# Retention and a bilinear feed-forward on one core: loading k and q of two pairs first, scaling the second pair on GpSimd, transposing q by parity

## The chip, the cores and the metric

The kernel runs on one core of one Trainium2 chip. Its time is device microseconds (us) of one execution; a time of a kernel is the median of its runs.

## The reference

A recurrent retention (linear attention with a decay for each head) is followed by a bilinear feed-forward. B = 4, H = 8, S = 768, D = 64; the feed-forward goes from 512 to 1536 and back.

```
gamma = 1 - 2 ** (-5 - arange(H));  scale = 1 / sqrt(D)
for t in range(S):
    state = gamma * state + outer(k[:, :, t], v[:, :, t])      # per batch and head, D x D
    y[:, :, t] = scale * q[:, :, t] @ state
x = y.transpose(0, 2, 1, 3).reshape(B * S, H * D)              # 3072 x 512
out = ((x @ w_a) * (x @ w_b)) @ w_out                          # float32
```

Inputs and outputs are float32.

## The kernel before

The 3072 rows are 24 slots of 128. The decay is put into k and q beforehand (`scaled`, line 210: k times one table of exponentials, q times another), so that the recurrence becomes plain linear attention: masked scores inside a chunk of rows (intra) plus q times a running state (inter).

The first six slots, all of batch 0, are worked as three *pairs* of 256 rows. A pair is loaded with even and odd rows side by side in one partition, so its two halves are a parity (`par`) each; c is the upper or lower half of the partitions, that is the first or second 128 rows of the pair. For a pair u the steps are:

- `casts2` scales k and q to bf16 (`kqb`) and casts v (`vb`)
- `flip2` transposes k or q on TensorE (line 384) through a PSUM tile `tp` and copies it to `kT2` or `qT2`
- `scores2` multiplies them (line 400, `at`), and VectorE multiplies the result by a mask (line 406, `aT`)
- `update2` adds k times v to the running state (line 419, `st`), and `keep_state` copies it for use as weights (line 428, `gbd`, on ScalarE)
- `intra2` and `inter2` sum masked scores times v and q times the state into two PSUM tiles `y` (lines 448 and 436), one for each c
- `leave2` copies these to `xt`, the feed-forward's input

The feed-forward `ffn_a`, `ffn_g` (lines 482 and 492) multiplies 128 columns of `w_a` or `w_b` by up to 512 rows of `xt`; ScalarE copies the one result (`asb`), VectorE multiplies the other by it (`ht`). `ffn_out` (line 519) is the second matrix product. The rows are cut into eight blocks (`TILES`); the first has the first two pairs, so the feed-forward cannot start until pair 0 and 1 have left. The 18 other slots are worked between feed-forward tiles.

Weights are loaded as float32 and cast by GpSimd (`cast_w`, `cast_o`). All loads are issued on one queue (SP) in the order of the list `LOADS`. `warm` issues matmuls of a zero tile whose result nobody uses (line 468), as filler on TensorE.

The order on every engine is the order in which the program text issues the work: `seq` chains each instruction to the one before it on its engine. PSUM tiles come from pools: `psff` has three buffers used in turn (tag `ff`: transposes, one of the two score sets, fillers, feed-forward), `psat` has one each for `at`, `y0` and `y1`, `psst` one for the state. A new tile waits until the old one in its buffer has been read.

Of the kernel before, what the change touches and what calls it, by code (L numbers as in the profile page):

```python
# [17 lines left out]
ON_PE = 8  # L18


LOADS = "p0 p1 w0 w1 w2 w3 w4 p2 w5 o0 o1 o2 o3 o4 o5 s6 s7 s8 s9 s10".split()


@with_exitstack
def kernel(
# [10 lines left out]
    nc = tc.nc  # L36
# [55 lines left out]
    def load_pair(u):  # L92
        for nm, src in (("k", k), ("q", q), ("v", v)):
            f = raw.tile([P, H, 2, D], F32, tag=nm + "f", name=nm + "f")
            s = src[0, :, 2 * u * P : 2 * (u + 1) * P, :].rearrange("h (p two) d -> p h two d", two=2)
            seq(nc.sync.dma_start(out=f, in_=s))
            for par in range(2):
                raws[nm, 2 * u + par] = f[:, :, par, :]

    def load_w(j):  # L100
        for nm, src in (("a", moe_w_a), ("b", moe_w_b)):
# [13 lines left out]
    def issue_loads(n):  # L115
        for _ in range(min(n, len(pending))):
            what = pending.pop(0)
            {"p": load_pair, "s": load_slot, "w": load_w, "o": load_o}[what[0]](int(what[1:]))


    kqb = {}
    issue_loads(6)
    zero = const.tile([P, 2 * P], F32, name="zero")
    seq(nc.vector.memset(zero, 0.0))  # L124
    lgr = const.tile([P, 1, H], F32, name="lgr")
    bq = const.tile([P, 1], F32, name="bq")
# [51 lines left out]
    def cast(engine, dst, src):  # L178
        if engine is nc.scalar:
            seq(nc.scalar.copy(dst, src))  # L180
        else:
            seq(engine.tensor_copy(dst, src))  # L182
# [182 lines left out]
    kT2, qT2 = {}, {}  # L365

    def casts2(u, on):
        for t in (2 * u, 2 * u + 1):
            new_nat(t)
        for (i, par), eng in on.items():  # L370
            scaled(eng, 2 * u + par, i)
        for t in (2 * u, 2 * u + 1):
            cast(nc.gpsimd, vb[t], raws["v", t])

    def flip2(u, i, on):
        if i == 0 and u not in kT2:
            kT2[u] = tra.tile([P, 2, HP, P], BF16, tag="kT2", name="kT2", bufs=2)
        if i == 1 and u not in qT2:
            qT2[u] = tra.tile([P, HP, P, 2], BF16, tag="qT2", name="qT2", bufs=2)
        for pars, eng in on:  # L380
            tp = psff.tile([P, 2, HP, P], BF16, tag="ff", name="tp")[:, : len(pars)]
            for m, par in enumerate(pars):
                for hp in range(HP):
                    seq(nc.tensor.transpose(tp[:, m, hp, :], kqb[2 * u + par][:, i, hp, :, :], ident))  # L384
            if i == 0:
                cast(eng, kT2[u][:, pars[0] : pars[0] + len(pars)], tp)
            else:
                cast(eng, qT2[u][:, :, :, pars[0]], tp[:, 0])

    def scores2(u, par, ff=False):  # L390
        t = 2 * u + par
        if not ff:
            both = psat.tile([P, 2, HP, P], F32, tag="at", name="at")
            at = [both[:, r] for r in range(2)]
        else:
            at = [psff.tile([P, HP, P], F32, tag="ff", name=f"at{r}") for r in range(2)]
        for hp in range(HP):
            for c in range(2):
                for r in range(2):
                    seq(nc.tensor.matmul(at[r][half(c), hp, :],  # L400
                                         kT2[u][half(r), par, hp, half(c)],
                                         qT2[u][half(r), hp, half(c), :],
                                         start=True, stop=True, skip_group_check=True))
        aT[t] = tra.tile([P, 2, HP, P], BF16, tag="aT", name="aT")
        for r in range(2):
            seq(nc.vector.tensor_tensor(aT[t][:, r], at[r], masks[par].to_broadcast([P, HP, P]),  # L406
                                        op=ALU.mult))
# [19 lines left out]
        for r in range(2):  # L427
            seq(nc.scalar.copy(gbd[1 - c][half(r), :, half(r)], state[0][half(r), :, :]))

    def inter2(u):  # L430
        for c in range(2):
            if (u, c) == (0, 0):
                continue
            for r in range(2):
                for hp in range(HP):
                    seq(nc.tensor.matmul(ys[u][c][half(hp % 2), 2 * r + hp // 2, :],
                                         gbd[c][:, hp, half(r)],
                                         qT2[u][:, hp, half(c), :], start=False, stop=False,
                                         skip_group_check=True))

    def intra2(u, par, begin):
# [10 lines left out]

    def leave2(u, on):
        J, i = where[2 * u]
        if i == 0:
# [9 lines left out]
    def warm(n, pool, tag):  # L465
        idle = pool.tile([P, 4 * P], F32, tag=tag, name="idle")
        for _ in range(n):
            seq(nc.tensor.matmul(idle[:, : 2 * P], zero[:, :P], zero, start=True, stop=True,  # L468
                                 skip_group_check=True))

    ht = {}
# [60 lines left out]
    K, Q = 0, 1  # L532
# [36 lines left out]
    ffn_a(0, 0, W2, 2 * W2)  # L569
    ffn_g(0, 0, 0, W2)  # L570
    ffn_g(0, 1, 0, W2)
    ffn_a(0, 1, W2, 2 * W2)
# [99 lines left out]
```

## Time and profile before

| | |
|---|---|
| median of 3 runs | 231.59 us (230.83 to 231.66) |
| the profiled execution's own time | 231.07 us |
| its span in the profile | 229.2 us |
| busy: TensorE, VectorE, ScalarE, GpSimd | 222.2, 97.9, 95.0, 78.0 us |
| moved by DMA | 39.19 MB, mean 171 GB/s |

In the rows PE is TensorE's matmuls, PEld its weight loads, DVE VectorE, ACT ScalarE, POOL GpSimd, SP the queue that issues the loads. L with a number is a line of the kernel; a helper (line 182 for copies on VectorE and GpSimd, 180 for those on ScalarE) stands for all its callers, so the tile names tell which copy it is. "xN" is a count; what stands in brackets is the engine's idle time before the instruction and what ended it. All times start with the span.

### The profile page before, as it was taken

How to read it: one execution, taken by the hardware profiler on the slowest of the kernel's cores; microseconds unless marked ns; L12 is line 12 of the kernel's file. 1: busy time of each engine (PE TensorE's matmuls, PEld its weight loads, DVE VectorE, ACT ScalarE, POOL GpSimd, SP SyncE). 2: the span in 40 equal slices, each digit the busy share in tenths (PEclk: the TensorE clock that was granted, in tenths of full speed). 3: DMA queues.
4: the chain of work that ended last, by engine and by line, in shares of the span. 5: the costliest groups of instructions: out<-in, count | busy, mean ns of one | idle time of the engine just before them, and what ended most of it. 6: DMA issues, size and time to landing. Idle time of an engine off the chain costs nothing.

```text
span 229.2 us, 6225 instructions
## 1 busy us (share of the span) xinstructions
PE 222.2 (97%) x2606; PEld 132.4 (58%) x2606; DVE 97.9 (43%) x193; ACT 95.0 (41%) x207; POOL 78.0 (34%) x101
## 2 busy tenths in 40 slices
PE   7989999999999999999989999999999999999994
PEld 6767445687446885885865454454445444444444
DVE  3695357645505552553565247460237310243300
ACT  3464426342427445445365336362335432433222
POOL 5568778787444444317086205000000000000000
PEclk9999999999999999999999999999999999999999
DMA  6999999999599998999999938002200002100022
GB/s 183 347 381 382 358 308 391 286 255 241 148 224 250 304 236 172 247 259 219 233 241 211 255 46 94 0 3 99 84 3 3 0 25 115 46 0 1 3 92 92
DMA packets 94011, 39.19 MB, mean 171 GB/s; under 512 B 73888, under 2 KB 89504, under 8 KB 93984
## 3 DMA queue, kind: packets, MB, share of 16 engines
q1 hardware_dynamic: 93840, 38.68, 67.0%
q8 instruction: 20, 0.33, 0.6%
q10 hardware_dynamic: 144, 0.13, 0.2%
q14 instruction: 7, 0.06, 0.1%
HBM read 28.31 MB, written 6.29 MB: 151 GB/s over the span
## 4 chain that ended last, share of the span: by engine, by line
PE 93%; DVE 4%; issue 1%; ACT 0%
PE o L519 27%; PE g L492 27%; PE a L482 27%; PE idle L468 3%; PE y L325 2%; PE y L336 1%; PE at L284 1%; DVE aT L406 1%; PE st L261 1%; DVE qT L182 1%; PE at L400 1%; DVE kqb L210 1%; PE y L448 1%; PE tp L384 1%; DVE aT L290 1%
## 5 line engine op out<-in xcount | busy, mean ns | idle before, releaser
L494 DVE TENSOR_TENSOR ht<-g,asb 128x256 bf16<-128x256 f32 (+1 forms) x98 | 53.7, 549 | 98.6 <-PE g L492 83.1
L482 PE MATMUL a<-xt,wa_bf 128*128 128x256 bf16 (+1 forms) x392 | 78.0, 323 | 1.3 <-DVE sums L275 0.5
L492 PE MATMUL g<-xt,wb_bf 128*128 128x256 bf16 (+1 forms) x392 | 77.5, 323 | 0.1
L485 ACT CAST asb<-a 128x256 bf16<-128x256 f32 (+1 forms) x98 | 46.4, 473 | 72.6 <-PE a L482 71.9
L519 PE MATMUL o<-wo_bf,ht 128*128 128x512 bf16 (+2 forms) x312 | 63.8, 363 | 0.0
L482 PEld LDWEIGHTS <-wa_bf 128*128 128x128 bf16 x392 | 37.6, 98 | 26.2 <-issue 1.0
L492 PEld LDWEIGHTS <-wb_bf 128*128 128x128 bf16 x392 | 38.3, 98 | 24.1 <-issue 0.4
L519 PEld LDWEIGHTS <-ht 128*128 128x128 bf16 x312 | 29.0, 98 | 31.4
L180 ACT COPY osb<-o 128x512 f32<-128x512 f32 (+2 forms) x25 | 14.1, 565 | 39.8 <-PE o L519 35.6
L210 POOL TENSOR_TENSOR kqb<-kf,ktab 128x512 bf16<-128x512 f32 x22 | 22.9, 1044 | 18.7 <-DMA kf<-in_k_dram 16.6
L182 POOL CAST vb<-vf 128x512 bf16<-128x512 f32 x24 | 15.4, 649 | 35.2 <-PE y L336 11.2
L210 POOL TENSOR_TENSOR kqb<-qf,qtab 128x512 bf16<-128x512 f32 x18 | 18.8, 1043 | 1.9 <-DMA qf<-in_q_dram 1.9
L180 ACT CAST gst<-sums 128x256 bf16<-128x256 f32 x33 | 12.9, 406 | 4.0 <-DVE sums L275 2.0
L275 DVE TENSOR_TENSOR sums<-st,sums 128x256 f32<-128x256 f32 x30 | 12.7, 423 | 1.4
L468 PE MATMUL idle<-zero 128*128 128x256 f32 x30 | 10.6, 493 | 1.3 <-DVE zero L124 1.3
L290 DVE TENSOR_TENSOR aT<-at,mask 128x512 bf16<-128x512 f32 x18 | 11.5, 679 | 0.0
L345 ACT CAST xt<-y 128x512 bf16<-128x512 f32 x18 | 9.7, 588 | 0.7 <-PE y L336 0.7
L468 PEld LDWEIGHTS idle<-zero 128*128 128x128 f32 x30 | 6.8, 245 | 2.5 <-DVE zero L124 1.2
L406 DVE TENSOR_TENSOR aT<-at,mask 128x512 bf16<-128x512 f32 x12 | 7.4, 681 | 1.0 <-PE at L400 1.0
L182 POOL CAST wb_bf<-wstb 128x1024 bf16<-128x1024 f32 (+1 forms) x7 | 6.9, 993 | 2.6 <-DMA wstb<-in_moe_w_b_dram 2.6
L182 POOL CAST wo_bf<-wsto 128x1024 bf16<-128x1024 f32 x6 | 6.2, 1042 | 1.9 <-DMA wsto<-in_moe_w_out_dram 1.9
L182 POOL CAST wa_bf<-wsta 128x1024 bf16<-128x1024 f32 (+1 forms) x7 | 6.4, 919 | 1.3 <-DMA wsta<-in_moe_w_a_dram 1.2
(54 smaller groups left out, 89.9 us busy)
## 6 DMA issues: line engine op xcount, KB each, us to landing
out_dram<-osb SPq DMA_DIRECT2D x23, 256.0 KB, 2.2
kf<-in_k_dram SPq DMA_DIRECT2D x18, 256.0 KB, 4.0
qf<-in_q_dram SPq DMA_DIRECT2D x18, 256.0 KB, 4.2
vf<-in_v_dram SPq DMA_DIRECT2D x18, 256.0 KB, 4.3
wsta<-in_moe_w_a_dram SPq DMA_DIRECT2D x6, 512.0 KB, 7.7
wstb<-in_moe_w_b_dram SPq DMA_DIRECT2D x6, 512.0 KB, 7.8
wsto<-in_moe_w_out_dram SPq DMA_DIRECT2D x6, 512.0 KB, 8.6
kf<-in_k_dram SPq DMA_DIRECT2D x3, 512.0 KB, 6.0
```

Source lines behind the costliest of these rows:

```text
L180: seq(nc.scalar.copy(dst, src))
L182: seq(engine.tensor_copy(dst, src))
L210: seq(eng.tensor_tensor(dst, src, tab, op=ALU.mult))
L275: seq(nc.vector.tensor_tensor(new, u[c][:, s], old, op=ALU.add))
L290: seq(nc.vector.tensor_tensor(aT[n][:, r].rearrange("p s h d -> p (s h) d"), at[:, r].rearrange("p s h d -> p (s h) d"), mask.to_broadcast ...
L345: seq(nc.scalar.copy(xt[J][:, :, i * P : (i + 2) * P].rearrange("p k (s c n) -> p c s k n", s=2, c=2)[:, c], ys[o][c]))
L468: seq(nc.tensor.matmul(idle[:, : 2 * P], zero[:, :P], zero, start=True, stop=True, skip_group_check=True))
L482: seq(nc.tensor.matmul(a, wa_bf[:, kt, fs], xcols(J, kt, c0, c1), start=(kt == 0), stop=(kt == KT - 1)))
L485: seq(nc.scalar.copy(asb, a))
L492: seq(nc.tensor.matmul(g, wb_bf[:, kt, fs], xcols(J, kt, c0, c1), start=(kt == 0), stop=(kt == KT - 1)))
L494: seq(nc.vector.tensor_tensor(ht[J][:, ft, c0:c1], g, asbs.pop((J, ft, c0)), op=ALU.mult))
L519: seq(nc.tensor.matmul(o, ht[J][:, ft, i * P : (i + 1) * P], wo_bf[:, ft, c0:c1], start=(ft == 0), stop=(ft == NFT - 1)))
```

## The change

- The loads of the first two pairs are issued tensor by tensor: k0, q0, k1, q1, v0, v1 instead of k0, q0, v0, k1, q1, v1. What follows is in the order of before.
- The second pair's q is scaled by GpSimd like its k, not by VectorE; the first pair's v is cast by ScalarE, not by GpSimd.
- The transposed q is kept with the two parities one behind the other, not interleaved. The masks follow with another pattern, and `leave2` puts the rows back in order with a strided write.
- The second pair's transposes and scores are issued before the first pair's intra, inter and leave steps. The first pair's state updates move behind the transposes of the second; its two leave copies are parted by an update and the inter step. For the second pair both intra sets come before the inter step and the last update, and the first two feed-forward groups come after the leave copies rather than among these steps.
- A filler matmul has 512 columns instead of 256 unless told otherwise, the zero tile is twice as long, and there are fewer fillers.
- In the first block, `ffn_a(0, 1, W2, ...)` moves ahead of `ffn_g(0, 1, 0, ...)`.

```diff
-LOADS = "p0 p1 w0 w1 w2 w3 w4 p2 w5 o0 o1 o2 o3 o4 o5 s6 s7 s8 s9 s10".split()
+LOADS = "k0 q0 k1 q1 v0 v1 w0 w1 w2 w3 w4 k2 q2 v2 w5 o0 o1 o2 o3 o4 o5 s6 s7 s8 s9 s10".split()
...
-    zero = const.tile([P, 2 * P], F32, name="zero")
+    zero = const.tile([P, 4 * P], F32, name="zero")
...
-                                        base=-par, pattern=[[0, 1], [1, P]],
+                                        base=-par, pattern=[[0, 1], [1, 2], [2, 64]],
...
         for (i, par), eng in on.items():
-            scaled(eng, 2 * u + par, i)
-        for t in (2 * u, 2 * u + 1):
-            cast(nc.gpsimd, vb[t], raws["v", t])
+            t = 2 * u + par
+            if i == V:
+                cast(eng, vb[t], raws["v", t])
+            else:
+                scaled(eng, t, i)
...
-            qT2[u] = tra.tile([P, HP, P, 2], BF16, tag="qT2", name="qT2", bufs=2)
...
+        into = (kT2, qT2)[i]
+        if u not in into:
+            into[u] = tra.tile([P, 2, HP, P], BF16, tag="kq"[i] + "T2", name="kq"[i] + "T2", bufs=2)
...
-                cast(eng, qT2[u][:, :, :, pars[0]], tp[:, 0])
+            cast(eng, into[u][:, pars[0] : pars[0] + len(pars)], tp)
...
-                                         qT2[u][half(r), hp, half(c), :],
+                                         qT2[u][half(r), :, hp, half(c)],
...
-            cast(eng, xt[J][:, i + c], ys[u][c])
+            if eng is None:
+                continue
+            cast(eng, xt[J][:, i + c].rearrange("p k (m par) -> p k par m", par=2),
+                 ys[u][c].rearrange("p k (par m) -> p k par m", par=2))
...
-    warm(6, psat, "y1")
+    warm(3, psat, "y1")
     casts2(0, {(K, 1): D_, (K, 0): D_, (Q, 0): D_, (Q, 1): D_})
+    casts2(1, {(K, 0): G_, (K, 1): G_, (Q, 0): G_, (Q, 1): G_})
+    casts2(1, {(V, 0): G_, (V, 1): G_})
+    cast_w(0, 2)
     flip2(0, K, [((1,), A_), ((0,), A_)])
-    warm(2, psat, "y1")
+    warm(1, psat, "y1")
     flip2(0, Q, [((0,), A_)])
-    warm(1, psat, "y1")
+    warm(1, psat, "y1", 2 * P)
     flip2(0, Q, [((1,), D_)])
-    warm(1, psat, "y1")
+    warm(1, psat, "y1", 2 * P)
     scores2(0, 1)
     scores2(0, 0, True)
+    warm(1, psat, "y1")
+    flip2(1, K, [((0, 1), A_)])
+    casts2(0, {(V, 1): A_, (V, 0): A_})
+    flip2(1, Q, [((0,), D_), ((1,), D_)])
     update2(0, 0)
-    warm(2, psat, "y1")
-    casts2(1, {(K, 0): G_, (K, 1): G_, (Q, 0): D_, (Q, 1): D_})
-    update2(0, 1)
-    intra2(0, 1, True)
-    inter2(0)
-    intra2(0, 0, False)
-    flip2(1, K, [((0, 1), A_)])
-    leave2(0, (A_, A_))
-    flip2(1, Q, [((0,), D_), ((1,), D_)])
-    warm(1, psff, "ff")
     scores2(1, 0, True)
     scores2(1, 1)
+    intra2(0, 1, True)
+    intra2(0, 0, False)
+    leave2(0, (A_, None))
+    update2(0, 1)
+    inter2(0, True)
+    leave2(0, (None, A_))
+    warm(1, psff, "ff")
     update2(1, 0)
-    cast_w(0, 2)
+    intra2(1, 0, True)
+    intra2(1, 1, False)
+    inter2(1, True)
+    update2(1, 1, False)
+    leave2(1, (A_, D_))
     W2 = 2 * P
-    warm(2, psff, "ff")
-    update2(1, 1, False)
-    intra2(1, 0, True)
-    inter2(1)
     ffn_a(0, 0, 0, W2)
-    intra2(1, 1, False)
-    leave2(1, (A_, D_))
     ffn_a(0, 1, 0, W2)
...
-    ffn_g(0, 1, 0, W2)
     ffn_a(0, 1, W2, 2 * W2)
+    ffn_g(0, 1, 0, W2)
...
-            casts2(2, {(K, 0): G_, (K, 1): G_})
+            casts2(2, {(K, 0): G_, (K, 1): G_, (V, 0): G_, (V, 1): G_})
```

More of the change, by code (lines that the diff above doesn't have):

```diff
@@ L90, in load_slot, with load_pair @@
             seq(nc.sync.dma_start(out=raws[nm, t], in_=s))
[L92 to L98, printed above, removed]
+    def load_pair(nm, u):
+        src = {"k": k, "q": q, "v": v}[nm]
+        f = raw.tile([P, H, 2, D], F32, tag=nm + "f", name=nm + "f")
+        s = src[0, :, 2 * u * P : 2 * (u + 1) * P, :].rearrange("h (p two) d -> p h two d", two=2)
+        seq(nc.sync.dma_start(out=f, in_=s))
+        for par in range(2):
+            raws[nm, 2 * u + par] = f[:, :, par, :]
     def load_w(j):
@@ L367, in casts2 @@
     def casts2(u, on):
-        for t in (2 * u, 2 * u + 1):
-            new_nat(t)
+        if 2 * u not in kqb:
+            for t in (2 * u, 2 * u + 1):
+                new_nat(t)
         for (i, par), eng in on.items():
-            scaled(eng, 2 * u + par, i)
-        for t in (2 * u, 2 * u + 1):
-            cast(nc.gpsimd, vb[t], raws["v", t])
+            t = 2 * u + par
+            if i == V:
+                cast(eng, vb[t], raws["v", t])
+            else:
+                scaled(eng, t, i)
     def flip2(u, i, on):
-        if i == 0 and u not in kT2:
-            kT2[u] = tra.tile([P, 2, HP, P], BF16, tag="kT2", name="kT2", bufs=2)
-        if i == 1 and u not in qT2:
-            qT2[u] = tra.tile([P, HP, P, 2], BF16, tag="qT2", name="qT2", bufs=2)
+        into = (kT2, qT2)[i]
+        if u not in into:
+            into[u] = tra.tile([P, 2, HP, P], BF16, tag="kq"[i] + "T2", name="kq"[i] + "T2", bufs=2)
         for pars, eng in on:
@@ L428, in keep_state, with inter2 @@
             seq(nc.scalar.copy(gbd[1 - c][half(r), :, half(r)], state[0][half(r), :, :]))
-    def inter2(u):
+    def inter2(u, last=False):
         for c in range(2):
@@ L437, in inter2 @@
                                          gbd[c][:, hp, half(r)],
-                                         qT2[u][:, hp, half(c), :], start=False, stop=False,
+                                         qT2[u][:, :, hp, half(c)], start=False, stop=last,
                                          skip_group_check=True))
@@ L454, in leave2 @@
         J, i = where[2 * u]
-        if i == 0:
+        if i == 0 and J not in xt:
             xt[J] = xtp.tile([P, 4, KT, P], BF16, tag="xt", name="xt")
         for c, eng in enumerate(on):
-            cast(eng, xt[J][:, i + c], ys[u][c])
+            if eng is None:
+                continue
+            cast(eng, xt[J][:, i + c].rearrange("p k (m par) -> p k par m", par=2),
+                 ys[u][c].rearrange("p k (par m) -> p k par m", par=2))
     def xcols(J, kt, c0, c1):
@@ L463, in xcols, with warm @@
         return xt[J][:, kt, c0:c1]
-    def warm(n, pool, tag):
+    def warm(n, pool, tag, w=4 * P):
         idle = pool.tile([P, 4 * P], F32, tag=tag, name="idle")
         for _ in range(n):
-            seq(nc.tensor.matmul(idle[:, : 2 * P], zero[:, :P], zero, start=True, stop=True,
+            seq(nc.tensor.matmul(idle[:, :w], zero[:, :P], zero[:, :w], start=True, stop=True,
                                  skip_group_check=True))
```

13 lines of the change are left out of this document (6 added, 7 removed).

## The prediction

> **What bounds the kernel now.** I read the page first, for the busy rows over the span and the chain that ended last.
>
> ```profile
> PE   7989999999999999999989999999999999999994
> PEclk9999999999999999999999999999999999999999
> PE 93%; DVE 4%; issue 1%; ACT 0%
> ```
>
> From about 20 us on TensorE does not stop, and its granted clock is full throughout. What the change edits is the head, before the feed-forward runs freely; a microsecond saved there moves everything behind it. So I read the chain of waits for the head (start, length, what):
>
> ```profile
> 8.78 0.74 DVE qT L182
> ...
> 9.57 0.45 PE at L400 x16
> ...
> 10.04 2.48 DVE aT L406 x4
> 12.52 1.61 DVE kqb L210 x2
> 14.14 1.27 DVE qT L182 x2
> ...
> 15.45 0.63 PE at L400 x30
> ...
> 19.53 0.70 DVE xt L182
> ...
> 20.27 0.61 PE a L482 x4
> ```
>
> From 10.04 to 15.4 VectorE is the bound without a break: it masks the first pair's scores, scales the second pair's q, copies its transposes. TensorE's 90% in those slices is partly the filler of line 468. My ruler is the start of feed-forward tile 2 (first line of the next fence): from there both kernels issue the same TensorE work. The timeline gives the TensorE prices (start, length, then engine, line, tiles, count):
>
> ```profile
> 22.91 1.89 PE L482 MATMUL a<-xt,wa_bf 128*128 128x512 bf16 x8
> ...
> 12.81 0.84 PE L384 MATMUL tp<-ident,kqb 128*128 128x128 bf16 x12
> ...
> 15.45 0.64 PE L400 MATMUL at<-qT,kT 64*64 64x128 bf16 x32 [0.21 <-DVE qT L182]
> 15.89 0.45 PE L419 MATMUL st<-vb,kqb 64*64 64x64 bf16 x16
> 16.26 1.13 PE L468 MATMUL idle<-zero 128*128 128x256 f32 x4
> 17.92 0.64 PE L436 MATMUL y<-qT,gbd 128*64 128x128 bf16 x16
> 18.49 0.61 PE L482 MATMUL a<-xt,wa_bf 128*128 128x256 bf16 x4
> 19.03 0.42 PE L448 MATMUL y<-aT,vb 64*64 64x128 bf16 x16
> 19.38 0.61 PE L482 MATMUL a<-xt,wa_bf 128*128 128x256 bf16 x4
> ```
>
> By start-to-start differences: scores of a pair (32) 0.44, a state update (16) 0.37, a full inter step (16) 0.57, one intra set (16) 0.35. Six 256-column feed-forward groups run from 20.27 to 22.91: 0.44 each.
>
> **The change part by part.**
>
> *The longer zero tile.* VectorE's memset of it doubles, and the fill waits for it:
>
> ```profile
> 0.93 0.27 DVE L124 MEMSET zero<- 128x256 f32 x1 [0.93 <-PEq L656]
> 1.25 5.15 PE L468 MATMUL idle<-zero 128*128 128x256 f32 x12 [1.25 <-DVE zero L124]
> 4.26 0.21 DVE L139 TENSOR_TENSOR earg<-posp,lgr 128x48 f32<-128x48 f32 x1 [2.02 <-POOL posp L136]
> 4.97 1.29 DVE L210 TENSOR_TENSOR kqb<-kf,ktab 128x512 bf16<-128x512 f32 x2 [0.50 <-ACT qtab L144]
> ```
>
> Three fills of 512 columns stream as many columns as six of 256, so TensorE's first transposes come 0.27 later. The later fills in front of the first scores are the same column counts, so the 0.27 reaches the second q transpose. GpSimd's mask selects get a pattern with one more dimension; earg and the first k scaling stand behind them, with the 0.50 of VectorE's idle time as cover. I cost it at nothing; without cover it would be what exceeds 0.50.
>
> *q transposed by parity.* The copies now write contiguously, and the leave copies (xt) take over the stride of two elements. Groups by form (count, then busy, mean ns):
>
> ```profile
> L182 DVE COPY qT<-tp 128x512 bf16<-128x512 bf16 x4 | 2.8, 726 | 1.6 <-PE tp L384 1.6
> L237 DVE COPY kqT<-tp 128x1024 bf16<-128x1024 bf16 x2 | 1.4, 692 | 0.0
> L180 ACT COPY qT<-tp 128x512 bf16<-128x512 bf16 x2 | 1.5, 736 | 0.3 <-PE tp L384 0.3
> L180 ACT COPY kT<-tp 128x512 bf16<-128x512 bf16 x2 | 1.1, 590 | 1.7 <-PE tp L384 1.7
> L180 ACT CAST xt<-y 128x512 bf16<-128x512 f32 x4 | 2.3, 593 | 0.0
> ```
>
> VectorE copied 1024 contiguous bf16 in 0.692, as long as 512 strided: a contiguous 512 lies between 0.35 and 0.73. I take 0.42, half the slope with its start-up. The first q copy then ends at 8.78 + 0.27 + 0.42 = 9.47 against 9.51, and the first scores start at 9.55 against 9.57: the late fill is paid back.
>
> For the strided xt copy on ScalarE there is no row. From below 0.59 (as before), by the strided q copy 0.736; a doubling, 1.18, as the far end. I take 0.736, the row with the same stride and engine. Two xt copies in a row took 1.08, so each is followed 0.49 after its start; strided, 0.63.
>
> [...]
>
> *Order of loads.* All six tensors are equally large, so k1 takes the first v's place, q1 the second k's, v0 the second q's. GpSimd shows when a place lands:
>
> ```profile
> 7.99 1.17 POOL L182 CAST vb<-vf 128x512 bf16<-128x512 f32 x2 [3.76 <-DMA vf<-in_v_dram]
> 9.62 2.04 POOL L210 TENSOR_TENSOR kqb<-kf,ktab 128x512 bf16<-128x512 f32 x2 [0.46 <-DMA kf<-in_k_dram]
> 12.53 2.08 POOL L182 CAST vb<-vf 128x512 bf16<-128x512 f32 x2 [0.86 <-DMA vf<-in_v_dram]
> ```
>
> So k1 is scaled 7.99 to 10.03 and q1 right behind it to 12.07, both on GpSimd; v0 lands near 11 (between 9.6 and 12.5). The weights keep their places. VectorE loses the 1.61 of q scaling.
>
> *The new head, step by step.* First scores 9.55; their 0.44 and one fill of 512 columns (as much as four passes; the row's 1.13 less the drain, 0.86): second k transposed at 10.85. From 12.81 of the transposes to the next row:
>
> ```profile
> 13.47 1.01 ACT L180 COPY kT<-tp 128x1024 bf16<-128x1024 bf16 x1 [0.80 <-PE tp L384]
> 14.38 1.08 ACT L180 CAST xt<-y 128x512 bf16<-128x512 f32 x2
> ...
> 10.50 0.76 ACT L428 CAST gbd<-st 64x256 bf16<-64x256 f32 x2 [1.73 <-PE st L419]
> ...
> L180 ACT CAST gst<-sums 128x256 bf16<-128x256 f32 x33 | 12.9, 406 | 4.0 <-DVE sums L275 2.0
> L485 ACT CAST asb<-a 128x256 bf16<-128x256 f32 x52 | 19.4, 373 | 27.7 <-PE a L482 27.0 <-DVE ht L494 0.6
> ```
>
> Hand-over 0.66, so the k copy starts at 11.51, and 0.91 later (13.47 to 14.38) ScalarE is free: 12.42. Now the two v casts, new on ScalarE. The pair gst and asb puts an SBUF source 0.03 above PSUM: about 0.62 each, 0.51 apart, done at 13.55 (bounds 13.4 and 13.9). VectorE meanwhile ends the masks at 12.50 and the two q copies near 13.4; q's transposes wait for the masks, as two of the three PSUM buffers hold the first scores.
>
> Behind the v casts TensorE stands still: update of pair 0 at 13.60, and queued behind it the second scores, at 13.97 instead of 15.45. Their masks run 14.44 to 16.92 (0.47 after the start as in 9.57 to 10.04, 2.48 long); the scores themselves are 1.48 earlier than before. This is the gross gain.
>
> Now ScalarE. How soon a leave copy follows its last intra set (which began at 19.03):
>
> ```profile
> 19.49 0.59 ACT L180 CAST xt<-y 128x512 bf16<-128x512 f32 x1
> ```
>
> The intra sets of pair 0 start at 14.41 and 14.76; 0.46 behind the last one's start the first half of xt leaves, at 15.22. Then in its queue: two state copies from 15.85 (0.39 apart), the second half of xt at 16.63, done 17.37. That copy frees the PSUM bank that the second pair's first intra set writes, so this set waits until 17.42, although its masks were ready. After it: two intra sets 0.70, inter 0.57, update 0.37: the feed-forward starts at 19.06. The second xt is ready near 19.55, under the first two groups, so all eight run through: 19.06 + 8 × 0.44 = 22.58. Against 22.91: 0.33 gained. Before, two of those groups were hidden in the wait for the second xt; now none is, which is the other 0.88 that the earlier masks don't bring.
>
> Weights cover this: their casts of the second tile ended here,
>
> ```profile
> 19.26 1.04 POOL L182 CAST wb_bf<-wstb 128x1024 bf16<-128x1024 f32 x1 [0.29 <-DMA wstb<-in_moe_w_b_dram]
> ```
>
> at 20.30, and tile 2 wants the gate half two 512-column groups after its start (22.58 + 2 × 0.88): 24.3. The third pair changes too: its q copies shorten and its xt lengthens by 0.15, between feed-forward groups of 0.88 that hide both. Nothing there.
>
> The profiled execution took 231.07 (span 229.2 and 1.87 around it): 230.74 after. The median of the runs, 231.59, stands 0.52 above that execution, so I forecast 231.3. A difference under 0.5% (1.16 us) I call no change, about what a measurement here can tell.
>
> **The rivals.**
>
> *A: ScalarE is not the new bound.* If the xt copies and hand-overs are short enough that only the second masks count, the last intra set starts at 16.97, then 0.35, 0.57, 0.37: feed-forward at 18.26, tile 2 at 21.78, 1.13 gained, 230.5; with intra sets at the pace of the scores (16 in 0.22) 0.13 more, 230.3. For it speaks ScalarE's share in this stretch (length, then busy PE, PEld, DVE, ACT, POOL):
>
> ```profile
> 15.00:20.00 5.00, 4.78 (x126) 3.41 (x124) 3.35 (x6) 2.06 (x5) 3.69 (x6) 1.00 1.09 383
> ```
>
> It was idle for 2.94 of 5. Against: the queue needs 2.15 from 15.22 to 17.37, and the cheaper xt price shortens that by 0.29, not by 0.8.
>
> *B, slower: the clock drops.* Between the second k transposes and the update (11.4 to 13.6) TensorE has only two sets of q transposes, 0.8 of 2.2, and no filler. In the rows above twelve passes of the first fill take 5.15, 0.43 each, and four later ones 1.13 with their drain: the early clock is about half. Were it half again from about 14, the TensorE work up to 16.7 (scores 0.44, intra 0.70, update 0.37, half an inter 0.28, fill 0.86, update 0.37: 3.0) would take 6, less some 0.8 of waits that vanish under it: 2.2 lost on the forecast's 231.3, 233.5. It decides if 1.4 us of idle time in some 3 us is enough. For it: nothing in before idles TensorE so much. Against: the granted clock never fell, also not over the shorter gaps of before.
>
> [...]
>
> *C: the strided xt is dearer than the strided q.* At the far end, 1.18, each of the two copies ahead of the second intra set costs 0.44 more: 0.9 together, 232.2. It would be a read of f32 with a strided write, of which there is no row.
>
> *D: the gain is given back,* because weights or loads pace tiles 2 to 9: 231.6. Against it the 4 us above.
>
> **How the numbers follow.** Forecast 0.42 (own range 230.9 to 231.7), A 0.24 (230.0 to 230.5), C 0.18 (231.6 to 232.9), D 0.05, B 0.11. The range from 230.1 to 232.6 leaves out B and the ends of A and C, under 0.2. Faster by over 0.5% (under 230.43): 0.20, most of A. Slower: B and 0.04 of C, 0.15. Within: 0.65.
>
> **What would show it.** Right: second scores near 14.0, ScalarE without gaps from 15.2 to 18, the first intra set of pair 1 released by an xt copy of some 0.74, tile 2 at 22.3 to 22.8. If that set is released by VectorE's masks, A; a cold clock row between 11 and 19, B; an xt copy near 1.2, C; GpSimd releasing TensorE after 22, D. Scores later than 14.5 would say that the v casts, or v's landing, were priced wrongly.

## The result, and the profile after

| | before | after |
|---|---|---|
| median time (6 runs each, same chip) | 231.42 us (230.83 to 231.78) | 234.99 us (232.97 to 235.82) |
| the profiled execution's own time, its span | 231.07, 229.2 us | 233.37, 231.3 us |
| start of feed-forward tile 2 in the profile | 22.91 us | 24.28 us |
| third pair's first scores (`at`) in the profile | 38.14 us | 40.33 us |

The ratio is 1.0141 (95% interval 1.0091 to 1.0191): the changed kernel is 1.4% slower. The forecast was 231.3, no change.

First the chain of waits of the changed kernel (start, length, what), as the prediction read it for the kernel before:

```profile
9.02 0.62 PE at L402 x32
...
11.19 1.01 ACT kT L183
12.20 1.04 ACT vb L183 x2
...
15.35 1.05 PE idle L473 x2
16.41 0.37 PE st L421 x16
16.78 0.56 PE y L450 x23
17.34 2.25 issue
19.58 0.32 PE y L450 x9
...
35.60 0.99 DVE kqb L213
...
36.76 1.52 DVE kqb L213
38.28 0.61 DVE ht L499
```

Two things are new in it. At 17.34 stands 2.25 us of "issue": TensorE waits for nothing that the profile shows, in the middle of the second pair's intra steps. And from 34.9 to 38.9 the chain runs over VectorE. In the kernel before it runs over TensorE and a copy on ScalarE there:

```profile
35.16 0.46 PE tp L384 x8
...
36.55 0.60 ACT asb L485
...
37.19 1.02 PE g L492 x4
```

Behind the first, tile 2 starts 1.37 late; between tile 2 and the third pair's scores another 0.82 is lost (16.05 instead of 15.23); then nothing more. Together 2.19, the difference of the spans (2.1).

The head up to 17 us went nearly as predicted. The timeline (start, length, engine, line, tiles, count, and what ended the idle time before), VectorE, ScalarE and TensorE in turn:

```profile
8.53 0.42 DVE L185 COPY qT<-tp 128x512 bf16<-128x512 bf16 x1 [0.94 <-PE tp L389]
...
13.99 2.48 DVE L408 TENSOR_TENSOR aT<-at,mask 128x512 bf16<-128x512 f32 x4 [0.83 <-PE at L402]
14.66 0.74 ACT L183 CAST xt<-y 128x512 bf16<-128x512 f32 x1
...
16.02 0.74 ACT L183 CAST xt<-y 128x512 bf16<-128x512 f32 x1
...
13.29 0.35 PE L421 MATMUL st<-vb,kqb 64*64 64x64 bf16 x11 [0.59 <-ACT vb L183]
...
16.61 0.72 PE L450 MATMUL y<-aT,vb 64*64 64x128 bf16 x23
19.58 0.32 PE L450 MATMUL y<-aT,vb 64*64 64x128 bf16 x9 [2.25 <-issue]
...
24.28 1.03 PE L487 MATMUL a<-xt,wa_bf 128*128 128x512 bf16 x4
```

The second pair's masks run from 13.99 (predicted 14.44), the xt copies take 0.74, the q copy 0.42, the update waits for ScalarE's v cast. Then the 32 matmuls of the two intra sets are cut in two, 23 and 9, though what they need was there: the last mask was done at 16.47, the second xt copy at 16.76. The weight loads stop with them: 24 before, the next at 19.58.

What moves in the gap is seen in the DMA view. For 16.5 to 19.7 us it lists, for the changed kernel, beside the loads

```profile
q8 instruction: 1, 0.02, 1.9%
```

(queue and kind, packets, MB, share). In the kernel before the same stretch has no such row. The packet is 16 KB, starts at 17.20, the first of its kind in the span, and takes 0.96; TensorE goes on 1.42 after its end. On the whole run there are 20 such packets for 5,184 recorded matmuls and weight loads of TensorE, one for about 259 of them; below I count a packet, or block, as 256 instructions, an estimate from these two numbers. And the stall falls behind exactly the 449th recorded instruction of TensorE (447 matmuls and weight loads, and two instructions at the very start). That is more than one block and less than two. My guess is that two blocks are used up there and the third has not come. The guess needs 63 instructions more, up to 512, that the trace does not record; no row shows these 63, and none shows how many blocks TensorE holds.

The second loss, VectorE and GpSimd, first after, then before:

```profile
35.52 2.76 DVE L213 TENSOR_TENSOR kqb<-qf,qtab 128x512 bf16<-128x512 f32 x2
35.26 1.04 POOL L185 CAST wb_bf<-wstb 128x1024 bf16<-128x1024 f32 x1 [0.93 <-DMA wstb<-in_moe_w_b_dram]
36.51 2.66 POOL L185 CAST wo_bf<-wsto 128x1024 bf16<-128x1024 f32 x2 [0.22 <-DMA wsto<-in_moe_w_out_dram]
```

```profile
34.15 1.40 DVE L210 TENSOR_TENSOR kqb<-qf,qtab 128x512 bf16<-128x512 f32 x2
34.90 1.55 POOL L182 CAST wb_bf<-wstb 128x1024 bf16<-128x1024 f32 x1 [0.49 <-DMA wstb<-in_moe_w_b_dram]
```

GpSimd's casts start when their weights land, within 0.4 us of the times before; VectorE's two scalings start 1.37 later, fall among the casts of w_b and w_out, and take 2.76 instead of 1.40. The next `ht` stands behind them, and TensorE behind that.

### The profile page after: what moved, and what is told of

Read it like the earlier page. It is cut to its first block, busy times and chain, and to the rows that moved or that the text cites. A ratio compares the mean times of both kernels' runs of the same rounds, so it can differ in the third digit from the quotient of the medians.

```text
span 231.3 us, 6196 instructions
## 1 busy us (share of the span) xinstructions
PE 221.0 (96%) x2592; PEld 129.4 (56%) x2592; DVE 97.1 (42%) x191; ACT 96.3 (42%) x209; POOL 78.1 (34%) x101
## 4 chain that ended last, share of the span: by engine, by line
PE 94%; DVE 2%; issue 2%; ACT 1%; DVEq 0%
PE o L524 27%; PE a L487 27%; PE g L497 27%; PE idle L473 4%; PE y L328 2%; PE y L339 1%; PE at L287 1%; DVE kqb L213 1%; PE st L264 1%; PE y L450 1%; PE tp L389 1%; PE st L421 1%; PE at L402 1%; PE y L438 1%; DVE ht L499 1%
## 5 line engine op out<-in xcount | busy, mean ns | idle before, releaser
L185 POOL CAST vb<-vf 128x512 bf16<-128x512 f32 x22 | 13.3, 610 | 29.3 <-PE y L339 23.6
L213 POOL TENSOR_TENSOR kqb<-qf,qtab 128x512 bf16<-128x512 f32 x20 | 20.8, 1042 | 1.7 <-DMA qf<-in_q_dram 1.6
L473 PE MATMUL idle<-zero 128*128 128x512 f32 (+1 forms) x16 | 9.4, 696 | 1.5 <-DVE zero L127 1.5
L185 POOL CAST wb_bf<-wstb 128x1024 bf16<-128x1024 f32 (+1 forms) x7 | 6.4, 918 | 3.4 <-DMA wstb<-in_moe_w_b_dram 3.4
L185 POOL CAST wo_bf<-wsto 128x1024 bf16<-128x1024 f32 x6 | 6.8, 1128 | 1.4 <-DMA wsto<-in_moe_w_out_dram 1.3
L328 PE MATMUL y<-kqT,gst 64*64 64x64 bf16 x264 | 5.8, 198 | 0.3 <-ACT lgr L305 0.3
```

The costliest lines, as they stand in the source:

```text
L213: seq(eng.tensor_tensor(dst, src, tab, op=ALU.mult))
L328: into(o, c, r, seq(nc.tensor.matmul(ys[o][c][half(hp % 2), s, 2 * r + j, :], gst[(2 * t + c) % 8][half(r), hp, :], kqT[t][half(r), 1, hp, ...
L473: seq(nc.tensor.matmul(idle[:, :w], zero[:, :P], zero[:, :w], start=True, stop=True, skip_group_check=True))
```

## The experiments

Two theories came from this. **F**, built on the guess: TensorE has two blocks, the third is asked for at the start of the second, and the request does not get past an instruction that waits. If so, in the changed kernel the wait for the v cast (the 160th recorded instruction) comes early, the request goes out only at 13.3, is served behind the queued loads, and TensorE uses up its second block first. No row shows a request; the runs can show only when the packet starts and where TensorE stalls. **P**: the later 0.82 is VectorE's scaling beside GpSimd's casts, a matter of when the two meet. The rivals are in the expectations. A ratio is always to the kernel before on the same chip, where that took 231.4 to 232.5 us.

**The changed kernel again**, with nothing edited.

> The changed kernel once more, with its clock in every execution. Its profile showed TensorE without an instruction from 17.1 to 19.6 us, just after its 449th, while an instruction block of 16 KB was moved at 17.2. Theory F (instruction fetch): the stall of 2 to 3 us is there again, at the same instruction, and tile 2 of the feed-forward starts near 24.3. Theory T (clock): the time above the kernel before follows the granted clock alone; an execution with a clock of 1.00 takes 231 to 232, one of 0.985 some 235. If both act, executions near 1.00 take 233 and the others more.

Measured: 235.93 us, ratio 1.0156 (1.0117 to 1.0195). The stall is again behind the 449th instruction, at the same matmul, though this execution's head ran 1.2 later (update at 14.47 instead of 13.29); the packet started at 18.24, 3.8 behind the update, as in the first profile (3.9).

```profile
20.62 0.32 PE L450 MATMUL y<-aT,vb 64*64 64x128 bf16 x9 [2.12 <-issue]
```

So the stall goes with the place in the program, not with the clock time. This trace also shows a granted clock that fell. Stretches of 3.41 us, the length at which the rows come out at 1.00 and 0.50, counted from the moment when the clock had first been full (span, then busy PE, PEld, DVE, ACT, POOL with counts, the granted clock, DMA share, GB/s):

```profile
17.80:21.21 3.41, 1.29 (x54) 0.93 (x50) 0.00 (x0) 0.86 (x3) 1.59 (x2) 1.00 1.09 380
21.21:24.62 3.41, 3.41 (x40) 2.50 (x35) 0.74 (x1) 1.48 (x3) 2.59 (x4) 0.50 1.10 389
24.62:28.04 3.42, 3.42 (x28) 2.56 (x27) 1.70 (x4) 1.50 (x5) 2.72 (x3) 1.00 1.11 348
```

In the stretch with the stall TensorE was busy for 1.29 of 3.41; the next stretch, exactly, had half the clock. From the end of the stall to tile 2 it is 6.23 us here (20.62 to 26.85) and 4.70 in the first profile (19.58 to 24.28), so the half clock cost 1.53, of the 1.7 that half speed over 3.41 us can cost. In the first profile the stall lay across a border of such stretches (1.95 busy in the one, 2.64 in the other), and no stretch was slowed:

```profile
15.39:18.80 3.41, 1.95 (x41) 0.90 (x42) 1.08 (x2) 2.06 (x6) 2.19 (x3) 1.00 1.09 380
18.80:22.22 3.42, 2.64 (x55) 2.27 (x55) 0.74 (x1) 1.47 (x3) 2.51 (x3) 1.00 1.09 384
```

Of the six runs of the result, the two with a mean clock of 0.998 or more took 232.97 and 233.37, the four with 0.985 to 0.993 took 234.46 to 235.82. That is about the difference between the median and the profiled execution (1.6).

**More instructions ahead of the wait (48 small first fills).** The fills are bf16 matmuls of a zero tile, 128 columns each (helper `small`); TensorE gets 84 more instructions before the wait.

```
-    warm(3, psat, "y1")
+    small(48, 128, 128)
```

> Three first fills of float32 become 48 bf16 matmuls of 128 columns: the same time on a cold TensorE, but 96 instructions instead of 12, so that every border of 256 instructions falls 84 instructions earlier in the program. Theory F: the second border then lies before the second pair's last state update and its block is asked for near 9.5 instead of 13.5; the stall is gone or under 0.5 us, tile 2 starts at 21.8 to 22.3, and the time is 230.3 to 231.5. Theory T, or a wait for data inside the intra sets: the stall stays where it is in the program, between the two halves of the second intra set, and the time is 233 or more.

Measured: 231.04 us, ratio 0.9954 (0.9926 to 0.9982). No stall; the packet started at 13.25, ahead of the update (13.70). Tile 2 started at 22.23.

```profile
17.02 0.83 PE L452 MATMUL y<-aT,vb 64*64 64x128 bf16 x32
```

**The same in the kernel before,** with 68 fills of 64 rows and 80 columns.

> The kernel before with its first six fills replaced by 68 small bf16 matmuls (64 rows, 80 columns): 136 instructions instead of 24, all in the idle time before the first k. Nothing else is changed. Theory F: the borders move 112 instructions forward, so that one falls where the second pair's scores start (near 15.5) and the next one near 20.3, 256 instructions and under 5 us later; TensorE stalls for 0.7 to 1.5 us near 20, and the time is 232 to 233. Theory T or any wait for data: the same time as before within 0.3 us, as no order and no wait is touched.

Measured: 233.37 us, ratio 1.0062 (1.0035 to 1.0088), slower, but with no stall. F's expectation, a stall near 20, missed. The 256 instructions behind the 449th took 5.7 us here (17.04 to 22.74), not under 5, and the next packet had started at 19.25, in time. What made the kernel slower is another thing: these small fills did not bring the clock up.

```profile
1.05 4.74 PE L476 MATMUL idle<-zb 64*64 64x80 bf16 x68 [1.05 <-DVE zb L124]
6.65 2.02 PE L470 MATMUL idle<-zero 128*128 128x256 f32 x4
...
12.13 1.13 PE L470 MATMUL idle<-zero 128*128 128x256 f32 x4
```

The same four passes took 2.02 at 6.65 and 1.13 at 12.13; the trace has the first full clock at 10.44 (5.92 in the profile before). The head was 1.6 to 1.7 later throughout. So this run does not test F where it was meant to, and it is no support for it.

**The same in the kernel before, with the 48 fills of the second run,** with which the clock was up in time (four passes took 1.08 at 6.88).

> The kernel before with its six first fills as 48 bf16 matmuls of 128 columns, as in e2: a control. Theory F: the borders of 256 instructions move by 72, none falls so that 256 instructions pass in less than the time of a block, and the time stays within 0.4 us of before. Rival: these fills are better in themselves (a warmer clock, an earlier start), and then this kernel gains about the 1 us that e2 had over the kernel before.

Measured: 233.53 us, ratio 1.0062 (1.0036 to 1.0088). More instructions at the start are thus no gain in themselves. The loss was expected by neither theory here. In the profile 1.08 of it is P's: tile 2 started at 23.29, the two scalings at 34.53 and took 2.98, and the stretch from tile 2 to the third pair's scores was 16.31 instead of 15.23. This execution, the slowest of its ten, lost another 2.6 behind these scores, and its chain shows most of that as gaps of TensorE for which the profile names no reason, far behind the head:

```profile
86.77 0.89 issue
...
106.17 1.44 issue
```

They stand at and behind dense rows of small matmuls, and TensorE goes on 2.6 and 2.4 after a 16 KB packet started (85.08 and 105.16). These are the signs of the stall in the head, in a kernel with the order of before.

**Loads held back.** The loads from the second weight pair on are issued only when ScalarE's v cast is done.

```
+            if (nm, j) == ("a", 1):
+                tc.add_manual_dep(bi.ins, last[mybir.EngineType.Activation].name, after, reason="late loads")
...
-    issue_loads(10)
+    issue_loads(7)
...
     update2(0, 0)
+    issue_loads(3)
```

> The changed kernel, with the loads of the weights from the second tile pair on held back until ScalarE has cast the first pair's v (near 13.3), so that fewer bytes are queued when TensorE asks for its block near 13.5. If the block waits behind queued data (theory D): it is moved by 15.5 instead of 17.2, the stall is under 1 us, and tile 2 starts near 23 unless the later weights hold it. If the block's delay has nothing to do with the queued loads: it is moved at 17.2 again, the stall stays 2.2 us, and the time is 233 to 235 or more as weights come later too.

Measured: 232.58 us, ratio 1.0011 (0.9985 to 1.0038). The update started at 14.46, no earlier than in the run of the unchanged one, and the packet at 15.62: 1.2 behind it, where 3.8 and 3.9 were measured with the loads queued. No stall, and tile 2 at 22.99, as expected if the instructions wait behind queued data:

```profile
17.79 0.83 PE L452 MATMUL y<-aT,vb 64*64 64x128 bf16 x32
```

So with the later loads held back the packet came sooner behind the wait, by 2.6 and 2.7, and in this execution the changed order costs no stall. Two of the ten executions, with a mean clock of 0.993, took 235.30 and 235.64; the ratio is of the other eight, and what happened in these two no trace shows.

**Twelve first fills of 128 columns for three of 512:** the same columns, in 36 more instructions.

```
-    warm(3, psat, "y1")
+    warm(12, psat, "y1", P)
```

> The changed kernel with its first fills as 12 matmuls of 128 columns instead of 3 of 512: the same work, 36 instructions more. Theory F: the stall stands again behind the 449th instruction of TensorE, which is now at the start of the second intra set's second half instead of inside it, and is shorter (1 to 2 us), as the block is asked for just ahead of the wait for v instead of behind it. A wait for data would stay at the same place in the program, that is behind the 485th.

Measured: **230.53 us, ratio 0.9942 (0.9913 to 0.9970)**, the lowest median of all kernels run, faster than both. From the update (13.32 for 13.29) to 16.4 us its head is that of the changed kernel to 0.03, but the packet comes at 13.89 instead of 17.20. F had expected a shorter stall, of 1 to 2 us; there is none:

```profile
13.32 0.35 PE L421 MATMUL st<-vb,kqb 64*64 64x64 bf16 x11 [0.89 <-ACT vb L183]
16.64 0.83 PE L450 MATMUL y<-aT,vb 64*64 64x128 bf16 x32
21.85 1.89 PE L487 MATMUL a<-xt,wa_bf 128*128 128x512 bf16 x8
```

From there to tile 2 the stall is the one difference, and it is worth 24.28 - 21.85 = 2.43 us at tile 2.

**Two thirds of that:** one fill of 512 columns and eight of 128, 24 instructions more, so that the wait for the v cast is the 184th.

```
-    warm(3, psat, "y1")
+    warm(1, psat, "y1")
+    warm(8, psat, "y1", P)
```

> The changed kernel with its first filler, three matmuls of 512 columns, cut into one of 512 and eight of 128: the same columns, 24 instructions of TensorE more (36 more, in the kernel with twelve of 128, removed the stall). Theory F (the request for the third block of instructions goes out at the 193rd recorded instruction, and cannot pass an instruction that waits): the wait for ScalarE's v cast moves from the 159th to the 183rd instruction, still ahead of the border. So the request still goes out only when the cast ends, near 13.3, the packet of instructions is moved near 17, and the stall of 2 to 2.5 us stays, after the 449th instruction, now some 24 earlier in the program, that is at the start of the second pair's intra sets; time 233 to 236. Rival (36 instructions helped because small matmuls at the start suit TensorE or its clock, or because the stall belongs to a place in the program): with two thirds of them the stall should shrink or vanish, packet at 14 to 15, 230.5 to 232; or the stall should stay at the 23rd matmul of the intra sets.

Measured: 232.32 us, ratio 1.0037 (1.0006 to 1.0068).

```profile
17.16 0.57 PE L450 MATMUL y<-aT,vb 64*64 64x128 bf16 x11
18.81 0.49 PE L450 MATMUL y<-aT,vb 64*64 64x128 bf16 x21 [1.08 <-issue]
```

The stall has moved 12 matmuls and their weight loads up in the program and is again behind the 449th instruction: it belongs to a count of instructions, not to a step. This is what F said. Its size is not: 1.1 instead of 2 to 2.5, because the packet came 2.5 behind the update (16.34 and 13.84), not 3.9; a stall that shrinks is what the rival had expected. Twelve instructions more, and it came 0.6 behind it. With the wait at the 160th, 184th and 196th instruction the packet thus came 3.9, 2.5 and 0.6 after the wait's end.

That the wait itself holds the request is not shown by this, as no run changes the wait alone. The 156th recorded instruction, which in all the changed kernels stands ahead of the wait, started 3.7 to 5.1 us before the packet in all 13 profiles with the loads queued, those of the kernel before among them, and 2.3 before it with the loads held back. A request that goes out about there, whatever waits behind it, and is delayed by the loads alone fits as well.

**Without the filler** ahead of the second pair's first update, from the kernel with twelve fills.

```
-    warm(1, psff, "ff")
     update2(1, 0)
```

> The changed kernel with twelve first fills of 128 columns (no stall, 230.53) without the filler matmul ahead of the second pair's first update. If ScalarE's second xt copy holds the second pair's intra sets, as the prediction had it, the filler only covers a wait: the intra sets start at the end of the xt copy (near 16.8) as before, and the time is within 0.2 of the kernel with the filler. If the filler itself is what is late, the update starts 0.5 to 0.8 earlier but the intra sets still wait for the xt copy, at most 0.3 gained: 230.2. If idle time of TensorE of this size lowers the clock (rival B of the prediction), a row of half clock follows near 17 to 21 and the time is 232 to 233.

Measured: 231.14 us, ratio 0.9975 (0.9946 to 1.0004), 0.6 over the kernel with the filler, where 0.2 was expected; the intervals overlap. By the profile the head is equal: from the first update to the second pair's inter step it is 4.08 here (13.55 to 17.63) and 4.09 with the filler (13.32 to 17.41). What the filler covered shows as two waits for ScalarE:

```profile
16.30 0.44 PE L421 MATMUL st<-vb,kqb 64*64 64x64 bf16 x16 [0.69 <-ACT gbd L430]
17.06 0.64 PE L450 MATMUL y<-aT,vb 64*64 64x128 bf16 x31 [0.26 <-ACT xt L183]
```

So ScalarE sets the head there, as predicted. The clock stayed full over these waits. The profile lost 0.8 behind the third pair's scores, most of it in another such gap (0.68 at 136.78; TensorE goes on 2.4 after a packet started at 135.04).

**The second pair's q scaled by VectorE again,** from the kernel with twelve fills.

```
-    casts2(1, {(K, 0): G_, (K, 1): G_, (Q, 0): G_, (Q, 1): G_})
+    casts2(1, {(K, 0): G_, (K, 1): G_})
...
     flip2(1, K, [((0, 1), A_)])
+    casts2(1, {(Q, 0): D_, (Q, 1): D_})
```

> The changed kernel with twelve first fills of 128 columns, but with the second pair's q scaled by VectorE, behind the masks of the first scores, as in the kernel before. The prediction's reading (VectorE was the bound of the head and lost 1.61 us of scaling): the second pair's q transposes come 1.0 to 1.6 later, its scores near 15, the feed-forward 0.8 to 1.2 later, time 231.3 to 231.8, that is the gain over the kernel before is gone. Rival (the gain comes from the order of the steps and the contiguous copies, and GpSimd's part is nothing): within 0.3 of 230.5.

Measured: 232.67 us, ratio 1.0046 (1.0011 to 1.0081).

```profile
14.17 0.40 PE L389 MATMUL tp<-ident,kqb 128*128 128x128 bf16 x4 [1.86 <-DVE kqb L213]
15.19 0.40 PE L389 MATMUL tp<-ident,kqb 128*128 128x128 bf16 x4 [0.62 <-DVE kqb L213]
```

TensorE waits for VectorE again. From the first scores to tile 2 it is 14.21 (10.18 to 24.39), against 12.80 with q on GpSimd: 1.4 us, the whole gain and more. The time is over the expected 231.3 to 231.8; the feed-forward came 0.2 later than the range allowed, and the third pair's scalings fell among the casts again (TensorE waits 1.65 there). This run also speaks against F's detail. Its packet started at 14.40, while the second wait held TensorE at the 187th until 15.19 and the 193rd (449 less the estimated 256) came after that: a request, if there is one, went out before this wait ended, some instructions ahead of what F takes for the first of the second block. How many, the runs don't settle.

**P by itself.** The third pair's q is scaled one step of the feed-forward sooner (3 us), in the kernel before, in the kernel with 48 fills, and in the changed kernel. GpSimd's work on the third pair moves with it in the program (the `casts2` line, its arguments not shown), but not in time: the first v cast of that pair starts at 31.80 with the edit and at 31.86 without.

```
+        if ft == 6:
+            casts2(2, ...)
+            scaled(D_, 4, Q)
+            scaled(D_, 5, Q)
         if ft == 7:
-            casts2(2, ...)
...
-        if ft == 7:
-            scaled(D_, 4, Q)
-            scaled(D_, 5, Q)
```

> The kernel before with nothing but the same earlier scaling of the third pair's q: a control for e5. There the two scalings took 1.40, hardly slowed, and the product of tile 8 followed at 35.47, with 0.9 of TensorE time lost near 36 to PSUM waits behind ScalarE. Theory P: 0.0 to 0.4 us faster, as only the wait for VectorE goes and ScalarE's stays. Rival: 0.7 or more faster, and then e5's gain is not the change's but this edit's.

> The kernel with 48 small first fills (e2), and the third pair's q scaled on VectorE one feed-forward round earlier, behind the product of tile 5 instead of tile 7, so that it runs near 30.1 to 31.7, mostly while GpSimd is idle. In e2 the two scalings took 2.14 us beside GpSimd's casts and held the product of tile 8 and with it TensorE for 0.85. Theory P (VectorE and GpSimd slow each other on such operations): the two scalings take 1.4 to 1.7, the wait is under 0.2, and the time is 230.0 to 230.6, 0.6 to 1.0 under e2. Rival: something else holds the third pair (its loads, PSUM), and the time stays at that of e2 within 0.3.

> The changed kernel with VectorE's scaling of the third pair's q one step of the feed-forward earlier (about 3 us), clear of GpSimd's casts of w_out; nothing ahead of 25 us is touched, so the stall stays. From the start of tile 2 to the third pair's scores it is 15.23 in the kernel before and 16.05 in the changed one. Theory P (the 0.82 between these is VectorE's scaling beside GpSimd's casts): the stretch falls to 15.2 to 15.4, the two scalings take 1.4 to 1.8 instead of 2.76, TensorE's wait of 1.10 for ht goes, and the time is 0.6 to 0.9 under that of the changed kernel: 234.1 to 234.4. Rival (something else is late there as well, as in the kernel with 48 fills, where the earlier scaling brought nothing): the stretch stays at 15.8 or more, 234.8 to 235.5.

Measured, with the runs above, by the profile (the stretch from tile 2 to the third pair's scores, and the length of the two scalings):

| kernel | scalings, us | stretch, us | ratio |
|---|---|---|---|
| before | 1.40 | 15.23 | |
| before, q sooner | 1.70 | 15.24 | 0.9987 (0.9953 to 1.0020) |
| before, 48 fills | 2.98 | 16.31 | 1.0062 (1.0036 to 1.0088) |
| changed | 2.76 | 16.05 | 1.0141 (1.0091 to 1.0191) |
| changed, q sooner | 1.28 | 15.24 | 1.0121 (1.0088 to 1.0155) |
| changed, loads held back | 1.28 | 15.24 | 1.0011 (0.9985 to 1.0038) |
| changed, twelve fills | 2.12 | 15.41 | 0.9942 (0.9913 to 0.9970) |
| changed, 48 fills | 2.14 | 15.44 | 0.9954 (0.9926 to 0.9982) |
| changed, 48 fills, q sooner | 1.80 | 15.24 | 0.9953 (0.9929 to 0.9977) |

In the changed kernel the sooner scaling gives back 0.81 of the 0.82: P holds. By the time this is seen only between executions of the same clock: both this kernel's profile and the one of the second run of the changed kernel had one slow stretch of 3.41 us, and their spans are 233.0 and 233.9. The median, 235.02, is over the expected 234.1 to 234.4, since by their mean clock (0.992 or 0.993) all six runs had such a stretch; this profile's is the same picture:

```profile
17.96:21.37 3.41, 1.38 (x54) 1.00 (x46) 0.00 (x0) 0.83 (x4) 1.57 (x2) 1.00 1.09 381
21.37:24.78 3.41, 3.41 (x36) 2.49 (x31) 0.74 (x1) 1.44 (x3) 2.59 (x4) 0.50 1.10 387
```

With 48 fills I had expected 0.6 to 1.0 and got nothing that the times show: there the collision cost only 0.2, and once VectorE is out of the way ScalarE's copies hold TensorE in the same place (chain of that kernel):

```profile
34.90 0.89 issue
35.78 0.60 ACT asb L498
```

In all five kernels whose scalings take 1.80 or less the stretch is 15.23 or 15.24, so the scaling has no more to give there.

## Why the prediction was wrong

**The step that failed** is "two intra sets 0.70, inter 0.57, update 0.37: the feed-forward starts at 19.06". The inter step and the update took the 0.57 and 0.37; the two intra sets took 3.13 (16.78 to 19.91), as 2.25 of stall fell into them. The sum let TensorE begin each instruction as soon as its operands were there: it had a term for each engine, each copy and each load of data, and none for the instructions themselves. Measured, that term is 2.43 at tile 2. The cause lies in the change all the same: behind the wait for ScalarE's v casts it puts a dense row of small matmuls with as many weight loads, so that the 290 instructions up to the 449th pass in 3.8 us (13.29 to 17.12). In the kernel before the same 290 took 7.3 us (10.17 to 17.47), and its packet came at 13.99, in time. That instructions were missing rests on the runs that moved the stall or took it away, with the packet's start 2.4 to 2.5 ahead of each end of it; what sets the moment of the packet stays open.

**The second step that failed** is "Nothing there", of the third pair: 0.82 was lost there. The rest of the way to the median, about 1.6, is by the runs' mean clocks the half clock behind the stall.

**The head itself** was right. From the first scores to tile 2 I had 13.03 (9.55 to 22.58); without the stall it is 12.80. The bound named, ScalarE's second xt copy, is the one that the run without the filler shows, and the 0.74 for a strided copy was exact, so rival C (1.18) falls. The first scores came 0.5 earlier than forecast, as the full clock was granted at 5.15 in this execution and at 5.92 in the profile before; over the executions here that moment lay between 4.8 and 7.7 with fills of 128 rows, and the head ran up to 1.2 later with it (update at 14.47 instead of 13.29). So of the 1.06 that the kernel with twelve fills gains at tile 2 (22.91 to 21.85), 0.33 is the forecast's, 0.2 shorter hand-overs, and 0.5 the early clock of that execution. In the times the kernels without a stall and with the new order (48 fills, twelve fills, twelve fills without the filler) stand 0.25 to 0.6% under the kernel before, the one with the loads held back 0.1% over it; I had 0.1% under. The 230.53 is what rival A would have given, but its mechanism (ScalarE not the bound) isn't there: the agreement is chance.

**Rival B** named half the clock, priced at 2.2, with 233.5 as its time. The half clock came, in four of six runs, but not by its road. The waits that it was built on did nothing (the run without the filler leaves even more of them); the instruction stall made one stretch of 3.41 us idle enough, and the following one paid 1.5. The condition that I gave it, "1.4 us of idle time in some 3 us", was too low: 1.86 idle in a stretch did not bring it, 2.03 and 2.12 did.

**Rival D** ("weights or loads pace tiles 2 to 9") was wrong in its means and right in its kind: 0.82 was given back at 35 us, because VectorE's work moved by 1.4 into GpSimd's casts. For the third pair I had looked at TensorE's cover and not at which engines meet.

**The chances.** Slower had 0.15, nearly all of it for B, and the range ended at 232.6. Both losses are of the sort that no single price holds: they depend on when a thing moved meets a thing that did not.

## What to carry to other kernels

When a change packs a dense run of small instructions into an engine's order, as here behind a wait, count the instructions up to it, and look up when the instruction packet starts. Here TensorE stood still behind its 449th where the packet came 2.5 to 3.9 us behind the end of that wait, and did not where it came 0.6 or 1.2 behind it; "issue" as the reason of a gap of TensorE, and an instruction packet beside it in the DMA view, were the signs. A few more instructions at the start, of the same work, can be all that is needed: here 36. And when work moves in time, ask of every later step what it now runs beside, not only whether it has slack.

## What the runs showed of the hardware that was not expected

- TensorE stalled for 1.1 to 2.3 us behind its 449th recorded instruction, in four profiles of three kernels, and went on 2.4 to 2.5 us after the start of a 16 KB packet of instructions, which itself took 0.96 in the changed kernel. Shorter gaps with the same signs stand far behind the head in four profiles, two of them with the order of before: 0.70 at 116.36 (changed), 0.89 at 86.77 and 1.44 at 106.17 (before, 48 fills), 1.03 at 138.55 (before, q sooner), 0.68 at 136.78 (no filler). Each ended 2.4 to 2.7 after a packet's start; that they too are missing instructions was not tested. With the loads queued the packet came up to 3.9 us after the end of the wait for the v cast; with the loads held back, 1.2.
- The granted clock fell to half for one stretch of 3.41 us where TensorE had been busy 1.29 (the changed kernel again) and 1.38 (q sooner) of the stretch before; behind one with 1.55 it stayed full, as the run with q on VectorE shows:

```profile
10.92:14.33 3.41, 1.55 (x13) 0.81 (x14) 3.41 (x6) 1.99 (x3) 1.76 (x3) 1.00 1.11 377
14.33:17.74 3.41, 2.65 (x113) 2.15 (x111) 2.75 (x5) 1.31 (x4) 2.50 (x5) 1.00 1.09 380
```

- VectorE's scaling (two inputs in SBUF) of two tiles took 1.28 (loads held back) to 1.40 (before) mostly clear of GpSimd's casts and up to 2.98 (before, 48 fills) beside them. Of the kernel before's 16 casts of 1024 columns 15 took 1.04; the one that began beside the scaling, at 34.90, took 1.55.
- A copy to bf16 on ScalarE with a stride of two elements took 0.74 for 512 columns and 0.59 without; VectorE's strided q copy of bf16 took 0.73, the contiguous one 0.42.
- 68 fills of 64 rows and 80 columns in 4.7 us did not bring the clock up: the stretch from 3.61 to 7.02 was busy throughout, and the clock was full only at 10.44. With the twelve fills of 128 rows and 128 columns it was full at 4.82.
